# A planned attention and mixture-of-experts kernel: more buffers for the first loads, a shared port that the planner always knows, pooling sums moved from GpSimd to VectorE, and a new table of priorities

## The chip, the core and the metric

The kernel runs on one core of a Trainium2 chip. Five engines work side by side and wait for one another through semaphores: TensorE (PE in the rows, with PEld for its weight loads), VectorE (DVE), ScalarE (ACT), GpSimd (POOL) and SyncE (SP), which here only issues transfers. The metric is the device time of one execution in microseconds (us), lower is better. Of several runs the median is taken.

## The reference

Two stages follow each other. The first is an attention whose keys and values are one and the same: a map of 384 x 32 positions with 128 channels is averaged over 4 x 4 windows to 768 keys and multiplied by a 128 x 128 matrix. The second sends each of the 49,152 output rows to one of 8 experts.

```python
B, N, C = 4, 384 * 32, 128
kv_pool = kv.reshape(B, H // 4, 4, W // 4, 4, C).mean(axis=(2, 4))
k = v = kv_pool.reshape(B, -1, C) @ w_sr                  # 768 keys for each batch
a = softmax(q @ k.transpose(0, 2, 1) / sqrt(C))
x = (a @ v).reshape(B * N, C)                             # 49152 rows
logits = normalized(x) @ normalized(expert_emb).T / tau   # 8 experts
e = argmax(logits); gate = softmax(logits)[e]
out[row] = gate * (relu(x[row] @ w1[e]) @ w2[e])          # inner width 1024
```

## The kernel before

**Tiles and steps.** Attention runs in 96 steps `k` of 512 query rows, 24 steps to a batch. A step has four blocks `j` of 128 rows. For each block TensorE makes the 128 x 768 scores `s` (`s_mm`, L717, six matmuls: the operands are held as a high and a low float16 part, and three of the four products are taken), VectorE takes the row maximum (`s_max`, L722), one of two engines turns it into a bias (`s_bias`, L732 on ScalarE or L734 on VectorE), and ScalarE writes the exponentials `p` (`s_exp`, L740). Then `p` is split into a high part (`p_hi`, L758 on ScalarE or L760 on VectorE) and a low part (`p_lo`, L768 on VectorE or GpSimd), both are transposed by transfers, and TensorE multiplies them with the values (`av`, L813). For some blocks of the first steps `p` is transposed by TensorE instead (L403) and copied back (L784, L786), a choice of the strings in a table. A step ends with a division (`x_norm`, `x_mul`, L832 on ScalarE or L834 on VectorE) and rows for the experts.

**Experts.** Every four steps a chain of small VectorE operations picks experts and places, and GpSimd scatters the rows to DRAM, 128 rows in each indirect transfer. An expert tile `t` of 512 rows of one expert reads them back transposed, and goes through eight units `u`: `l1` (L1430, three matmuls of 512 columns into `ph`), `h_hi` on ScalarE (L1437, writes `hh`), `h_lo` on VectorE (L1442, writes `hl`), then `l2` (L1466 with `hh`, eight matmuls) and `l2_lo` (L1466 with `hl`, four). All eight units add up in one bank `po`, which VectorE empties in `o_out` (L1476). Its rows go out by scatters on GpSimd.

**Keys.** For batch 0 the map comes in 16 loads of 96 x 1024 numbers (`kv_load_0`, L455): four groups `h`, each of four rows `i` that VectorE adds up (`kv_sum_0`, L460; then `kv_cols_0`, L466 and L467). Seven buffers named `kvt0` hold them. For the other batches the map comes in eight loads of four rows each, added on GpSimd for batch 1 (`kv_adds`, L428) and by two VectorE reductions for batches 2 and 3 (`kv_window`, L446). From the pooled map TensorE makes the keys; a largest absolute value then gives their scale (for batch 0 in `kv_max_0`, L487).

**What sets the order.** Nothing is written in the order in which it runs. Every operation is handed to a planner with an engine, a duration, a priority (`key`) and what it depends on. `Plan.run` then plays the kernel through while it is built: the engine that is free first takes, of its ready operations, the one of lowest priority number, and the operation is put out then. So the durations and priorities in the code decide the fixed order of each engine's queue, and nothing else. The table `X` holds the offsets of the priorities and the strings that choose engines. Some operations carry `port=True`: GpSimd and VectorE are taken to hold one port in turn, but before the change only after 350 us of planned time (`X["pt"]`).

Of the kernel before, what the change touches and what calls it, by code (L numbers as in the profile page):

```python
# [33 lines left out]
P_LO = {"D": 0.96, "P": 1.65}  # L34
# [6 lines left out]
    ka=23, da=5.5, di=12.584, db=9.582, dma=1.426, ahead=2.462, av=10.242, av0=-0.17054466704045357, lb=0.8,  # L41
    l2=1.712, qt=5.48, lead=15.491, x=2.408, r=3.279, s=-1.285, p=9.158, x0=5.936, r0=8.101, s0=1.53, p0=5.53,
    qt0=0.531, pm="cabcbcacccbccbcacadcdad", pl="aaaaaaaa", nm="DDAAA", xn="ADAA", nm0="DDA", xn0="DA",
    we="dcdadcddaddcddcd", h=4.264, kv=6.773, kvs=0.752, w0=-14.986, start=22.623, early=22.314,
    wd=13.772691170763045, xw=1.904, qd=29, qs=7.744, ql=5.509,
    em="---------M-M-M-M-M-M-M-M-M-M-M-M-M-M-M-M-M", et=0.715, ec=0.5, v0=82.796, sd=0, qu=1.602, q0=-38.113,
    avd=0.262, m=1.928, end=-1.35, ne=-6.946, ge=-32, pt=350.0, kd=(2, 3), gap=1.8,
# [4 lines left out]
def attention_moe(  # L52
# [162 lines left out]
    LAT["~", "ACT"] = X["xw"]  # L215

# [15 lines left out]
    class Plan:  # L232
# [13 lines left out]
        def chain(self, key, step, fns, *deps, dur=0.17, eng="DVE", port=False):  # L246

            ops = []
            for i, fn in enumerate(fns):
                ops.append(self.add(eng, dur, key + i * step, fn, *(deps if not ops else ops[-1:]), port=port))  # L250
            return ops
# [14 lines left out]
        def run(self, begin):  # L266

            soon, now, free = {}, {}, {}
            held = dict(DVE=0.0, POOL=0.0)
# [20 lines left out]
            while any(count):  # L290
# [28 lines left out]
                if op.port and t > X["pt"]:  # L319
                    other = held["POOL" if eng == "DVE" else "DVE"]  # L320
                    if other > t + 0.1:
                        rest = [x for x in now[eng] if not x[2].port and self.can_go(x[2])]
                        rest = [x for x in rest if not (scatters(x[2]) and t < paced + X["gap"])]
                        if rest:
                            x = min(rest)
                            now[eng].remove(x)
                            now[eng].append((op.key, i, op))
                            heapq.heapify(now[eng])
                            op = x[2]
                        else:  # L330
                            t = other
# [110 lines left out]
    def kv_window(b, h, i):  # L442
        if i == 0:
            kv_pooled(b, h)
# [1511 lines left out]
```

## Time and profile before

| | us |
|---|---|
| median of 3 runs | 2136.58 |
| lowest and highest run | 2129.0, 2136.97 |
| the profiled execution, its own time | 2133.14 |
| span in its trace, first to last instruction | 2131.4 |
| TensorE busy | 1961.6 (92%) |
| VectorE busy | 1738.8 (82%) |
| ScalarE busy | 1551.0 (73%) |
| GpSimd busy | 1263.2 (59%) |
| mean granted clock of TensorE, as a share of full speed | 0.984 |

A share of the whole span is a mean over unlike stretches, so the rows below cut it: up to the first scores at 46 us, attention alone up to some 380 us, attention and expert tiles together up to some 1800 us, and experts alone at the end. Busy time of an engine includes time in which an instruction has begun and is held up.

### The profile page before, as it was taken

Reading aid. Unit: us, or ns where it says so; the run is one execution under the profiler, and the core shown is the slowest. Engines: PE = TensorE matmul, PEld = TensorE weight load, DVE = VectorE, ACT = ScalarE, POOL = GpSimd, SP = SyncE. Lnnn points to the kernel's source line nnn. Section 1 sums busy time; section 2 is a strip of 40 time slices with the busy share of each in tenths; the row PEclk is TensorE's granted clock in tenths of the full one; section 3 lists DMA queues with packets and bytes.
Section 4 is the critical chain, followed back from the end, with each engine's and each line's share of the span. In section 5 each row is a group of like instructions: output and inputs, shape, how many; then the busy total and the mean of one; then the engine's idle time right before and its main releaser. Section 6 shows DMA issues by size and latency. Waiting matters only on the chain. (4 is left out here: it accounts for less than half of the span.)

```text
span 2131.4 us, 57911 instructions
## 1 busy us (share of the span) xinstructions
PE 1961.6 (92%) x21396; PEld 1500.0 (70%) x21396; DVE 1738.8 (82%) x3711; ACT 1551.0 (73%) x3256; POOL 1263.2 (59%) x1744
## 2 busy tenths in 40 slices
PE   3777888899999999999999999999999999999997
PEld 1556676676776777677777777677777776776687
DVE  7989788789998888999988888788888887565554
ACT  3977788787877778688888887787888886543333
POOL 1558654566666667656557667656666656656333
PEclk9989899999999999999999999999999999999999
DMA  8987554999999999899888799797879777432242
GB/s 236 193 214 195 137 106 95 205 183 181 169 179 177 168 172 181 178 184 186 151 157 158 143 161 185 147 161 147 156 145 164 145 133 133 83 80 61 47 106 53
DMA packets 844545, 322.66 MB, mean 151 GB/s; under 512 B 792659, under 2 KB 804060, under 8 KB 842465
## 3 DMA queue, kind: packets, MB, share of 16 engines
q1 hardware_dynamic: 817184, 264.13, 67.1%
q0 software_dynamic: 24704, 53.53, 9.5%
q8 instruction: 170, 2.79, 0.5%
q10 hardware_dynamic: 2368, 1.25, 0.2%
q14 instruction: 119, 0.97, 0.2%
HBM read 170.55 MB, written 64.50 MB: 110 GB/s over the span
## 5 line engine op out<-in xcount | busy, mean ns | idle before, releaser
L1442 DVE SCALAR_TENSOR_TENSOR hl<-ph,hh 128x512 f16<-128x512 f32 x740 | 506.4, 686 | 176.4 <-ACT hh L1437 131.6
L190 POOL DMA_INDIRECT out_dram<-o,m x388 | 411.5, 1061 | 400.0 <-DVE o L1476 109.8
L1430 PE MATMUL ph<-x,wbuf 128*128 128x512 f16 (+1 forms) x2328 | 601.4, 370 | 21.4 <-DVE hl L1442 12.5
L1437 ACT ACTIVATE hh<-ph 128x512 f16<-128x512 f32 x740 | 439.3, 595 | 241.7 <-PE ph L1430 161.2
L190 POOL DMA_INDIRECT xs_rows<-rows,pi x384 | 429.0, 1117 | 214.8 <-issue 31.8
L1466 PE MATMUL po<-wbuf,hh 128*128 128x128 f16 x5920 | 452.5, 219 | 34.4 <-DVE o L1476 16.7
L717 PE MATMUL s<-k,qT 128*128 128x512 f16 (+1 forms) x2304 | 442.1, 331 | 32.1 <-ACT p L740 22.0
L740 ACT ACTIVATE p<-s,nm,qa 128x768 f32<-128x768 f32 x384 | 380.0, 991 | 98.5 <-DVE nm L734 71.8
L1466 PEld LDWEIGHTS <-hh 128*128 128x128 f16 x6208 | 381.3, 98 | 65.4 <-issue 30.1
L722 DVE TENSOR_REDUCE nm<-s 128x1 f32<-128x768 f32 x384 | 363.7, 948 | 28.2 <-PE s L717 17.7
L768 DVE TENSOR_TENSOR plo<-p,phi 128x768 f16<-128x768 f32 x339 | 339.5, 1002 | 25.0 <-ACT phi L758 16.0
L717 PEld LDWEIGHTS <-qT 128*128 128x128 f16 x2304 | 218.2, 99 | 166.5 <-issue 45.8
L1430 PEld LDWEIGHTS <-wbuf 128*128 128x128 f16 x2544 | 227.1, 98 | 144.3 <-issue 29.6
L813 PE MATMUL xp<-v,pthi 128*128 128x137 f16 x4200 | 313.0, 224 | 4.5 <-DVE w L600 1.3
L1466 PEld LDWEIGHTS <-hl 128*128 128x128 f16 x3104 | 228.7, 98 | 109.7 <-issue 3.3
L813 PEld LDWEIGHTS <-pthi 128*128 128x128 f16 x4200 | 274.8, 98 | 40.1 <-issue 6.1
L758 ACT CAST phi<-p 128x768 f16<-128x768 f32 x345 | 286.8, 832 | 6.9 <-issue 2.4
L1466 PE MATMUL po<-wbuf,hl 128*128 128x128 f16 x2960 | 286.4, 219 | 0.3 <-issue 0.2
L813 PE MATMUL xp<-v,ptlo 128*128 128x137 f16 x2100 | 187.2, 224 | 2.2 <-DMA ptlo<-plo 2.0
L813 PEld LDWEIGHTS <-ptlo 128*128 128x128 f16 x2100 | 142.0, 98 | 3.1 <-DMA ptlo<-plo 2.4
L846 POOL TENSOR_TENSOR rows<-x,rows 128x512 f16<-128x512 f32 x96 | 113.3, 1180 | 41.2 <-ACT rows L841 40.5
L861 ACT ACTIVATE junk<-x 128x128 f32<-128x128 f32 x384 | 116.3, 311 | 6.1 <-DVE x L834 5.1
(358 smaller groups left out, 1958.4 us busy)
## 6 DMA issues: line engine op xcount, KB each, us to landing
wbuf<-w_prep SPq DMA_DIRECT2D x106, 1026.0 KB
q<-in_q_dram SPq DMA_DIRECT2D x96, 256.0 KB
kvt<-in_kv_dram SPq DMA_DIRECT2D x24, 768.0 KB
wf<-in_moe_w_dram SPq DMA_DIRECT2D x16, 512.0 KB
out_dram<-o,m POOLq DMA_INDIRECT x388
kvt<-in_kv_dram SPq DMA_DIRECT2D x16, 384.0 KB
xs_rows<-rows,pi POOLq DMA_INDIRECT x384
w_prep<-wo SPq DMA_DIRECT2D x8, 514.0 KB
```

The costliest lines, as they stand in the source:

```text
L190: ins = nc.gpsimd.indirect_dma_start(out=dst[:, :], out_offset=bass.IndirectOffsetOnAxis(ap=idx, axis=0), in_=src, in_offset=None, bounds_ ...
L717: nc.tensor.matmul(t[:, lo:hi], qs[:, l, :], r[:, lo:hi], start=i == 0, stop=i == 2)
L722: V.tensor_reduce(out=nm, in_=ks[k]["s", j], axis=AX.X, op=ALU.max, negate=True)
L740: nc.scalar.activation(out=p, in_=ks[k].pop(("s", j)), func=AF.Exp, bias=ks[k].pop(("nm", j)), scale=ks[k]["fac"],)
L758: nc.scalar.copy(out=hi, in_=p)
L768: eng.tensor_tensor(out=lo, in0=ks[k].pop(("p", j)), in1=hi, op=ALU.subtract)
L813: nc.tensor.matmul(ks[k]["xp", h][:, i, :w], l[:, c, :], r[:, c, :w], start=n == 0, stop=n == len(terms) - 1)
L861: nc.scalar.activation(out=junk, in_=ks[k]["x"][:, j, 0:C], func=AF.Square, accum_out=groups[g]["ss"][:, i * NQ + j : i * NQ + j + 1],)
L1430: nc.tensor.matmul(ph[:, kk * n : (kk + 1) * n], wt[:, o + f : o + f + P], r, start=i == 0, stop=i == 2)
L1437: nc.scalar.activation(out=hh, in_=ts[t]["ph", u], func=AF.Relu)
L1442: V.scalar_tensor_tensor(out=hl, in0=ts[t].pop(("ph", u)), scalar=0.0, in1=ts[t]["hh", u], op0=ALU.max, op1=ALU.subtract)
L1466: nc.tensor.matmul(ts[t]["po"][:, j * C : (j + 1) * C], h[:, kk * n + j * P : kk * n + (j + 1) * P], wt[:, f : f + P], start=u == 0 and i ...
```

## The change

Six things change.

1. Of batch 0's 16 loads, the four of group `h = 1` use the four buffers `wf` of the experts' weights, and the last of group 3 uses `wo0`; the other eleven share the seven `kvt0`.
2. The planner applies the shared port from the start, on more operations (a list of names, `SHARED`, and more `port=True`), with a small gap after the other engine's hold, and a TensorE operation that begins after more than 2.05 us of idle time is planned as slower for a while.
3. The sums of the map for batches 1 to 3 are four additions on VectorE; GpSimd's five and VectorE's reductions are gone.
4. Durations: `p_lo`, the scatters, the copies, transposes and others are given other numbers.
5. New offsets and engine strings in `X`. Over the whole kernel, 89 of the bias operations move from VectorE to ScalarE, 36 of the divisions `x_mul` move there too (two instructions each on ScalarE, one on VectorE), and 45 of `p_hi` move from ScalarE to VectorE. Five steps (24 to 28) turn their queries by transfer and not by TensorE, which is 20 transposes of 128 x 128 fewer.
6. The chain that picks experts for the first three groups has an earlier priority, and the first selection of tiles runs on VectorE.

```diff
-P_LO = {"D": 0.96, "P": 1.65}
+P_LO = {"D": 0.9, "P": 1.62}
+SHARED = (
+    "halve", "guess", "square", "times", "update", "norm", "guard", "logits", "shift", "hits", "onehot", "pick", "cast",
+    "gate", "same", "take", "power", "floor", "after", "until", "divide",
+)
+KV_ADD = {"D": (1.13, 0.6, 0.33, 0.2), "P": (2.4, 1.25, 0.7, 0.45)}
...
-    l2=1.712, qt=5.48, lead=15.491, x=2.408, r=3.279, s=-1.285, p=9.158, x0=5.936, r0=8.101, s0=1.53, p0=5.53,
+    ka=23, da=6.087, di=12.327, db=9.098, dma=1.67, ahead=2.284, av=9.354, av0=0.067, lb=-0.963, l2=2.044, qt=8.333,
...
-                if op.port and t > X["pt"]:
-                    other = held["POOL" if eng == "DVE" else "DVE"]
-                    if other > t + 0.1:
...
                 if op.port:
-                    held[eng] = t + op.dur
-                op.end = t + op.dur
+                    mate = "POOL" if eng == "DVE" else "DVE"
+                    if held[mate] > t + 0.02:
+                        op.ready = asked[eng] = held[mate] + PORT[eng]
+                        put(op)
+                        continue
...
+                took = op.dur
+                if eng == "PE":
+                    if t - free.get(eng, 0.0) > 2.05:
+                        cold = t + 3.4
+                    took += max(min(op.dur, (cold - t) / 2), 0.0)
+                op.end = t + took
...
         return [
-            lambda: add(row(0), row(0), row(1)), lambda: add(row(2), row(2), row(3)),
-            lambda: add(row(0), row(0), row(2)), lambda: add(cols(0, 2), cols(0, 2), cols(2, 4)),
-            lambda: add(lambda: kv_pooled(b, h), cols(0, 1), cols(1, 2)),
+            add(rows(0, 2), rows(0, 2), rows(2, 4)), add(rows(0, 1), rows(0, 1), rows(1, 2)),
+            add(cols(0, 2), cols(0, 2), cols(2, 4)), add(lambda: kv_pooled(b, h), cols(0, 1), cols(1, 2)),
         ]
...
+    KV_BUFS = dict(kvt0=7, wf=4, wo0=1)
+
+    def kv_tag(h, i):
+        return "wf" if h == 1 else "wo0" if h == i == R - 1 else "kvt0"
...
-            if b in X["kd"]:
-                for i in range(2):
-                    r = add("DVE", 1.2, t0 + 8.0 + 0.2 * i, lambda h=h, i=i: kv_window(b, h, i), o, r, *deps)
-                    reads("kvt", r)
...
+            on = X["kd"][b - 1]
+            for i, fn in enumerate(kv_adds(b, h, V if on == "D" else nc.gpsimd)):
+                r = add(ENG[on], KV_ADD[on][i], t0 + 8.0 + 0.1 * i, fn, o, r, *deps, port=True)
+                reads("kvt", r)
```

How the change moves instructions is seen at three places.

**The start of SyncE's queue.** Here stand the loads of batch 0's map (`kvt_h_i`) and of the first queries (`q`), from the seventh row on. Before:

```order
L455 DMA kvt_1_2_193<-in_kv_dram 96x1024
L636 DMA q_197<-in_q_dram 128x512
L636 DMA q_199<-in_q_dram 128x512
L636 DMA q_206<-in_q_dram 128x512
L455 DMA kvt_1_3_213<-in_kv_dram 96x1024
L455 DMA kvt_2_0_217<-in_kv_dram 96x1024
L455 DMA kvt_2_1_224<-in_kv_dram 96x1024
L455 DMA kvt_2_2_238<-in_kv_dram 96x1024
L636 DMA q_244<-in_q_dram 128x512
```

And now, from the same place of the same queue:

```order
L468 DMA kvt_1_2_192<-in_kv_dram 96x1024
L468 DMA kvt_1_3_196<-in_kv_dram 96x1024
L468 DMA kvt_2_0_201<-in_kv_dram 96x1024
L468 DMA kvt_2_1_210<-in_kv_dram 96x1024
L468 DMA kvt_2_2_214<-in_kv_dram 96x1024
L468 DMA kvt_2_3_218<-in_kv_dram 96x1024
L468 DMA kvt_3_0_222<-in_kv_dram 96x1024
L468 DMA kvt_3_1_230<-in_kv_dram 96x1024
L649 DMA q_234<-in_q_dram 128x512
L468 DMA kvt_3_2_240<-in_kv_dram 96x1024
L468 DMA kvt_3_3_244<-in_kv_dram 96x1024
```

Before, six loads of queries stand ahead of the last load of the map, and now one does. The first two loads of expert weights follow the map's in both orders, now with one more load of queries between.

**One unit of an expert tile on TensorE.** In the long middle stretch, tile 11, from `l1` of unit 3 (`ph11_3`) to `l2` of the same unit (`hh11_3`); `hl11_1` is the low part of unit 1, and so on. One row stands for each run of matmuls. Before:

```order
L1430 MATMUL ph11_3_9497<-x_11_8486,wbuf2_4559 128x512
...
L1466 MATMUL po11_9469<-wbuf2_4559,hl11_1_9433 128x128
...
L1466 MATMUL po11_9469<-wbuf2_4559,hh11_2_9465 128x128
...
L1430 MATMUL ph11_4_9535<-x_11_8486,wbuf2_4559 128x512
...
L1466 MATMUL po11_9469<-wbuf2_4559,hl11_2_9478 128x128
...
L1466 MATMUL po11_9469<-wbuf2_4559,hh11_3_9525 128x128
```

And now (`s_0` are scores of attention):

```order
L1443 MATMUL ph11_3_9408<-x_11_8372,wbuf2_4404 128x512
...
L1479 MATMUL po11_9386<-wbuf2_4404,hh11_1_9289 128x128
...
L1479 MATMUL po11_9386<-wbuf2_4404,hl11_1_9317 128x128
...
L730 MATMUL s_0_159<-k0_1_4954,qT34_8903 128x512
...
L1443 MATMUL ph11_4_9447<-x_11_8372,wbuf2_4404 128x512
...
L1479 MATMUL po11_9386<-wbuf2_4404,hh11_2_9397 128x128
...
L1479 MATMUL po11_9386<-wbuf2_4404,hl11_2_9412 128x128
...
L1443 MATMUL ph11_5_9473<-x_11_8372,wbuf2_4404 128x512
...
L1479 MATMUL po11_9386<-wbuf2_4404,hh11_3_9426 128x128
```

Before, `l2` of unit 3 follows its `l1` after one other unit's `l1`, and between `hh` and `hl` of a unit lies an `l1`. Now `l2` follows after two other units' `l1` and a block of scores, and `hl` comes right behind `hh`. Of the 352 units of tiles 30 to 73 none stood nearer before than this one, and at least a tenth as near; now 95 in 100 stand at least as far apart as this one.

**The seam between two expert tiles on TensorE.** From the last matmuls of tile 10 (`hl10_7`) to the first `l2` of tile 11 (`hh11_0`), which needs the bank `po` that `o_out` of tile 10 has emptied. Before:

```order
L1466 MATMUL po10_9057<-wbuf1_4558,hl10_7_9341 128x128
...
L1430 MATMUL ph11_2_9441<-x_11_8486,wbuf2_4559 128x512
...
L717 MATMUL s_0_159<-k0_1_3981,qT34_8866 128x512
...
L1466 MATMUL po11_9469<-wbuf2_4559,hh11_0_9343 128x128
```

And now (`xp32_0` is a half step of `av`, 36 matmuls):

```order
L1479 MATMUL po10_8965<-wbuf1_4403,hl10_7_9245 128x128
...
L826 MATMUL xp32_0_9296<-v0_1_108,pthi32_0_8705 128x137
...
L826 MATMUL xp32_0_9296<-v0_1_108,ptlo32_0_8738 128x137
...
L730 MATMUL s_1_160<-k0_1_4954,qT34_8903 128x512
...
L1443 MATMUL ph11_2_9379<-x_11_8372,wbuf2_4404 128x512
...
L1479 MATMUL po11_9386<-wbuf2_4404,hh11_0_9267 128x128
```

Before, 9 matmuls lie in between, and now 45. Of the 44 seams of tiles 30 to 73 nearly all were like this one before; now three in four are, and the narrowest are as narrow as before.

## Rows read from the trace of the kernel before

**Rows 1.** Busy time by stretch: PE, PEld, DVE, ACT, POOL, granted clock, DMA share, GB/s.

```profile
0.00:30.00 30.00, 5.95 (x18) 3.51 (x18) 19.65 (x58) 11.35 (x24) 3.26 (x27) 1.00 0.95 246
...
46.00:380.00 334.00, 272.30 (x2269) 213.41 (x2268) 285.70 (x613) 260.64 (x539) 197.73 (x225) 0.92 0.69 160
...
400.00:1800.00 1400.00, 1356.70 (x15338) 1028.15 (x15338) 1221.44 (x2621) 1117.26 (x2386) 888.61 (x1264) 1.00 0.89 164
1800.00:2132.00 332.00, 303.87 (x3592) 239.69 (x3588) 186.78 (x368) 141.28 (x265) 158.84 (x206) 0.99 0.34 74
```

**Rows 2.** Timeline of the start: begin, duration (us), engine, line, what, idle before.

```profile
22.00 3.03 SPq L455 DMA_DIRECT2D kvt<-in_kv_dram  x5
...
34.39 1.22 DVE L460 TENSOR_TENSOR kvt<-kvt,kvt 96x1024 f32<-96x1024 f32 x1 [0.17 <-DMA kvt<-in_kv_dram]
...
39.98 0.55 DVE L487 TENSOR_REDUCE m<-s 128x1 f32<-128x384 f32 x1
...
45.89 0.80 PE L717 MATMUL s<-k,qT 128*128 128x512 f16 x2 [0.91 <-ACT k L523]
```

**Rows 3.** Who TensorE waited for, 46 to 380 us, then 400 to 2132.

```profile
PE s L717 <- ACT p L740: 20.6, 17, 2.6
...
PE po L1466 <- DVE o L1476: 16.7, 26, 2.0
PE po L1466 <- ACT hh L1437: 13.9, 20, 2.7
```

**Rows 4.** VectorE's groups, 46 to 380 us: busy us, mean ns, idle before.

```profile
L768 DVE TENSOR_TENSOR plo<-p,phi 128x768 f16<-128x768 f32 x46 | 49.9, 1085 | 4.9 <-ACT phi L758 4.1 <-issue 0.7
...
L665 DVE TENSOR_SCALAR qa<-qa,ksc 128x2 f32<-128x2 f32 x10 | 12.2, 1219 | 0.0
...
L1053 DVE TENSOR_TENSOR wo<-w 128x4 f32<-128x4 f32 x7 | 6.2, 889 | 0.0
```

**Rows 5.** Single lines, whole span: ns least/median/greatest, first and last start us.

```profile
L768 DVE TENSOR_TENSOR plo<-p,phi x339: 895/950/2717, 59.7 to 1828.7; 128x768 f16<-128x768 f32 x170
...
L665 DVE TENSOR_SCALAR qa<-qa,ksc x48: 207/221/4728, 44.6 to 1713.0; 128x2 f32<-128x2 f32 x48
...
L1053 DVE TENSOR_TENSOR wo<-w x8: 142/158/2097, 42.7 to 253.7; 128x4 f32<-128x4 f32 x8
...
L446 DVE TENSOR_REDUCE pooled<-kvt x32: 1867/1916/1952, 457.4 to 1041.1; 96x64 f32<-96x1024 f32 x32
...
L466 DVE TENSOR_TENSOR kvt<-kvt x4: 670/686/689, 12.3 to 35.6; 96x512 f32<-96x512 f32 x4
```

**Rows 6.** GpSimd's sums of the map for batch 1, 46 to 380 us.

```profile
L428 POOL TENSOR_TENSOR kvt<-kvt 96x512 f32<-96x512 f32 (+1 forms) x32 | 36.5, 1142 | 0.6
```

**Rows 7.** TensorE's timeline in the middle stretch; the spacing of starts is read.

```profile
801.15 0.81 PE L1430 MATMUL ph<-x,wbuf 128*128 128x512 f16 x3
801.80 0.39 PE L1466 MATMUL po<-wbuf,hl 128*128 128x128 f16 x4
802.03 0.61 PE L1466 MATMUL po<-wbuf,hh 128*128 128x128 f16 x8
802.47 1.14 PE L717 MATMUL s<-k,qT 128*128 128x512 f16 x6
803.45 0.89 PE L813 MATMUL xp<-v,pthi 128*128 128x137 f16 x12
...
804.54 0.81 PE L1430 MATMUL ph<-x,wbuf 128*128 128x512 f16 x3
```

**Rows 8.** Groups of the whole span that the table of engines moves or removes.

```profile
L403 PE MATMUL pq<-ident,q 128*128 128x128 f32 x116 | 18.6, 287 | 9.6 <-ACT q L671 5.4 <-DVE x L834 1.8 <-ACT x L832 1.4
...
L758 ACT CAST phi<-p 128x768 f16<-128x768 f32 x345 | 286.8, 832 | 6.9 <-issue 2.4
...
L732 ACT ACTIVATE nm<-nm,scales,qa 128x1 f32<-128x1 f32 x206 | 79.3, 385 | 51.1 <-DVE nm L722 42.7 <-issue 5.5 <-DVE qT L697 0.9
...
L832 ACT ACTIVATE x<-xp,rn 128x136 f32<-128x136 f32 x266 | 84.6, 371 | 48.8 <-DVE rn L824 30.3 <-DVE wo L1053 3.5 <-DVE rn L823 3.3
```

More of the change, by code (lines that the diff above doesn't have):

```diff
@@ L318, in run @@
                     continue
-                if op.port and t > X["pt"]:
-                    other = held["POOL" if eng == "DVE" else "DVE"]
-                    if other > t + 0.1:
[L322 to L331, printed above, removed]
-                if op.port:
-                    held[eng] = t + op.dur
-                op.end = t + op.dur
+                if op.port:
+                    mate = "POOL" if eng == "DVE" else "DVE"
[3 more added lines that the diff above has]
+                        continue
+                    rest = [x for x in now[eng] if not x[2].port] if eng == "POOL" and asked[mate] > t else []
+                    rest = [x for x in rest if self.can_go(x[2]) and not (scatters(x[2]) and t < paced + X["gap"])]
+                    if rest:
+                        x = min(rest)
+                        now[eng].remove(x)
+                        now[eng].append((op.key, i, op))
+                        heapq.heapify(now[eng])
+                        op = x[2]
+                    else:
+                        asked[eng] = 0.0
+                        held[eng] = t + op.dur
+                took = op.dur
[4 more added lines that the diff above has]
+                op.end = t + took
                 free[eng] = op.end
@@ L422, in kv_pooled, with kv_adds, rows @@
         return st[b]["pooled"][:, h, :]
-    def kv_adds(b, h):
+    def kv_adds(b, h, eng):
         def add(out, in0, in1):
-            nc.gpsimd.tensor_tensor(out=out(), in0=in0(), in1=in1(), op=ALU.add)
-        def row(i):
-            return lambda: st[b]["kvt", h][:, i, :]
+            return lambda: eng.tensor_tensor(out=out(), in0=in0(), in1=in1(), op=ALU.add)
+        def rows(lo, hi):
+            return lambda: st[b]["kvt", h][:, lo:hi, :]
         def cols(lo, hi):
@@ L1529, in kv_rows_0 @@
             for i in range(R):
-                o = took("kvt0", add("SP", 0.45, t0 + i, lambda h=h, i=i: kv_load_0(h, i), *turn("kvt0", 7), dma=1.3))
+                tag = kv_tag(h, i)
+                room = turn(tag, KV_BUFS[tag])
+                o = took(tag, add("SP", 0.45, t0 + i, lambda h=h, i=i: kv_load_0(h, i), *room, dma=1.3))
                 if i == 0:
-                    first, tile = o, len(uses["kvt0"]) - 1
+                    first, tile = o, uses[tag][-1]
                 else:
@@ L1809, in group_ops @@
             t -= X["ge"]
+        if g < 3:
+            t -= X["gk"]
         ops = g_logits(g)
-        lg = chain(
-            t, 0.3, ops, *counted[g], *placed.get(g - 1, ()), *placed.get(g - 2, ()), dur=0.22 if g > 3 else 0.17, port=True,
-        )
+        lg = chain(t, 0.3, ops, *counted[g], *placed.get(g - 1, ()), *placed.get(g - 2, ()))
         t += 0.3 * len(ops)
@@ L1828, in group_ops @@
         sc = [
-            add("POOL", 1.37, t + 1.37 * i, lambda i=i: g_scatter(g, i), pc[-1], gc[-1], dma=0.22) for i in range(GT)
+            add("POOL", 1.12, t + 1.37 * i, lambda i=i: g_scatter(g, i), pc[-1], gc[-1], dma=0.22) for i in range(GT)
         ]
```

88 lines of the change are left out of this document (45 added, 43 removed).

## The prediction

> **What bounds the kernel now.** I read the busy time by stretch first, then TensorE's waits, then VectorE's groups where TensorE is idle. The reader is to see three stretches with three different limits [rows 1]. From 400 to 1800 us TensorE is busy for 1356.7 of 1400 us: it is the bound, and only 43.3 us are idle there. At the end, 1800 to 2132, 28.1 us are idle. From 46 to 380, attention alone, it is busy for 272.3 of 334 us, so 61.7 us are idle, and its mean granted clock is 0.92, between its two levels of 1.2 and 2.4 GHz, after stretches in which it stood idle. At full clock those 272.3 us would be some 272.3 x 0.92 = 250.5, so the low level costs about 22 us more. No engine is full in that stretch: VectorE is at 285.7 of 334 (86%), ScalarE at 260.6 (78%). They wait for one another. Ahead of it the start costs 45.9 us until the first scores [rows 2].
>
> So the most that an order could give back is 61.7 + 22 in the first stretch, 43.3 + 28.1 behind it, and part of the start. The TensorE work itself hardly changes.
>
> **The start.** The first scores come at 45.89, 11.5 us after the last addition of batch 0's map begins at 34.39 [rows 2], and that addition waits for its transfer. The five last loads are issued only from 22.00 on. Ahead of the last load's landing the queue has 16 loads of 96 x 1024 x 4 bytes and six of queries of 128 x 512 x 4 bytes, 7.86 MB; at the 246 GB/s of the first 30 us [rows 1] this is 32.0 us, and the addition begins 2.4 us after that. Now one load of queries stands ahead: 6.55 MB, 26.6 us, and with the same 2.4 us the addition begins at 29.0, 5.4 us sooner. VectorE can follow: twelve additions of 1.22 us [rows 2] and four of 0.69 [rows 5] with smaller ones behind are under 20 us from the first landing on. But the largest of the keys (39.98 before) is queued on VectorE behind the two maxima of the first expert's weights, in both orders. Their loads land after 6.55 + 0.26 + 1.05 = 7.86 MB, which is one load of queries later than the map, and two query subtractions now stand there as well. The weights' loads now also wait until group 1 of the map has left their buffers; its additions end before the map's last load lands, so I count nothing. I take 4 of the 5.4 us. The bounds are 0, if the queries or VectorE's queue then come last, and 6.
>
> **The first stretch.** Here instructions of VectorE are held up. L665 works on two numbers per partition. Its median is 0.221 us and its longest 4.728 [rows 5], while its mean in this stretch is 1.219 [rows 4]. L665, L768 and L1053 together: 10 x (1.219 - 0.221) + 46 x (1.085 - 0.950) + 7 x (0.889 - 0.158) = 10.0 + 6.2 + 5.1 = 21.3 us of holding-up. These three alone are 6% of the stretch, and the plan for it counted none, since its port rule began at 350 us of planned time. GpSimd's additions, 36.5 us in 32 instructions of 1.14 us [rows 6], stand right there and are removed. VectorE gets in return eight times four additions: 1.22, 0.69, and two smaller ones that no row shows, bounded by 0 and 0.69 each. Going by halves (0.35, 0.20) a load costs 2.46 us and the batch 19.7. Up to the first expert unit VectorE's queue has 32 bias operations fewer (at 0.207, the least of L665, 6.6 us) and 8 high parts more (between 0 and 0.95, the median of L768; I take half, 4 us). So VectorE's own work grows by 19.7 - 6.6 + 4 = 17 us, and it has less to do only if more than 17 of the 21.3 us go. That would be worth little by itself.
>
> What I expect is less waiting by TensorE: its largest wait here is for the exponentials that free a score tile, 20.6 us in 17 waits [rows 3], and they come late when a VectorE instruction ahead of the maximum or the bias is held up. Shorter idle time also keeps the clock up. The price lies between a loss of the 17 us (over VectorE's 86% share, 20) and a gain of half of the 61.7 + 22. I take a gain of 10, an eighth of it, because VectorE's own work grows, and because the old plan already got 82% from a wrong rule.
>
> **Behind it.** Two of TensorE's waits go by the distances in its queue. The seam: `l2` waits for `o_out`, 16.7 us in 26 waits, the longest 2.0 [rows 3]. Nine matmuls fill it before, one block of `l1` and one of scores: 0.65 + 0.98 = 1.63 us by their spacing [rows 7]. Now two blocks of `av` stand there too, (804.54 - 803.45) = 1.09 each, so 3.81 us. That is 2.18 us more, above the longest wait. The unit: `l2` waits for `hh`, 13.9 us in 20 waits, the longest 2.7. Before, 0.23 + 0.44 + 0.65 + 0.23 = 1.55 us of matmuls lie between `l1` and `l2` of a unit; now 0.44 + 0.23 + 0.98 + 0.65 + 0.44 + 0.23 + 0.65 = 3.62, that is 2.07 more. So nearly all of the 30.6 us could go. `hl` now comes right behind `hh`, but with 3.62 + 0.44 = 4.06 us after its `l1`, where VectorE has its time. What is late next: a faster TensorE asks more of VectorE (1221 of 1400 us, 87%) and ScalarE (80%) [rows 1]. ScalarE gets some 60 bias operations at 0.385 and 72 division parts at 0.371, and loses some 35 high parts at 0.832 [rows 8]: 23.1 + 26.7 - 29.1 = 21 us more, 81% of the 1400. VectorE loses what these were there, and two reductions of 1.916 for each load of batches 2 and 3 [rows 5], 30.7 us a batch against 19.7. No engine becomes the bound, but their queues are full enough to be late elsewhere. I take half of the 30.6, 15; the bounds are 0 and 31.
>
> Twenty transposes of queries fewer on TensorE, at 18.6 / 116 = 0.16 us [rows 8]: 3 us. The transfers that take their place stand in SyncE's queue steps ahead. The earlier experts' chain and the first selection on VectorE cost nothing that I can find: TensorE's queue has the first expert unit behind the same attention work as before.
>
> **A rule weighed.** The reductions of batches 2 and 3 show no holding-up: 1867 to 1952 ns in 32 instructions. An operation with two inputs in SBUF, L768, shows it: 895 to 2717 [rows 5]. The Trainium skill (SBUF — State Buffer, Who interferes with whom) states that a reduction never contends with GpSimd, while an addition of two SBUF inputs is blocked by a GpSimd instruction that reads SBUF; the rows agree. By that rule alone, were each of the 64 additions of these batches to meet a whole GpSimd sum of 1.14 us, VectorE would stand 73 us longer in its 1400, at 91% in place of 86% (1221 - 22 + 73), and the waits of TensorE that I count as gone would come back: the forecast would be 15 us higher. By L768's own excess in the first stretch, 0.135 us, the 64 cost 9 us on an engine that isn't the bound, and the sum stays as it is. I follow the row.
>
> **Sum.** 4 + 10 + 15 + 3 = 32 us. The profiled execution took 2133.1, so 2101; that execution lies 3.4 us below the median of 2136.58 and inside the three runs, and I leave the forecast at 2101.
>
> **Rivals.**
> *VectorE bounds the first stretch, slower.* The additions bring 17 us of work, and the weights' low parts, rows and scatters of GpSimd keep holding the port, so the 21.3 us stay. At VectorE's 86% share the stretch grows by 17 / 0.86 = 20 us, and the waits behind it return nothing. 2133 + 20 - 4 - 3 = 2146. It decides when less than 17 of the 21.3 us go. For it: VectorE is the fullest engine there. Against: GpSimd's 32 sums, 36.5 us, are gone from that stretch [rows 6]. Chance 0.13. The Trainium skill's rule above, on additions of two inputs, is the mechanism.
> *Nothing but the transposes counts.* The start is given back, since the attention alone then waits for exponentials as before, and at the seam `hl` or the scores come late in place of `o_out` and `hh`. 2133 - 3 = 2130. For it: VectorE and ScalarE are at 80 to 87%, and an engine works its queue in order. Against: both distances grew by more than the mean of the waits (0.64 and 0.70 us). Chance 0.20.
> *The first stretch heals.* Idle time and low clock feed each other, and half of 61.7 + 22 goes, with all of 30.6: 2133 - 4 - 42 - 31 - 3 = 2053. For it: no engine is full there. Against: VectorE gets 17 us more of its own work. Chance 0.15.
>
> **How the numbers follow.** The forecast, 2101, has 0.52, with 2085 to 2117 as its own range. For 8 in 10 I go down to 2066, halfway to the healing case, and up to 2140, which takes in the case of no effect and leaves out half of the slower one. A change of 0.5% (11 us) is what a measurement of this kernel can tell from none: faster than 2126 or slower than 2147. Faster: 0.52 + 0.15 and a quarter of the 0.20, 0.72. Slower: half of the 0.13 and a little of the rest, 0.10. Same: 0.18.
>
> **What would show it.** First scores near 42 us. In the stretch after it, L665 near its median of 0.221 and TensorE's idle time under 55 us, with the granted clock above 0.92. Between 400 us and the end, waits for `o_out` and `hh` under 15 us together. I'd be wrong if VectorE's instructions are held up for as long as before, or if `hl` takes over the waits.

## The result and the profile after

| | before | after |
|---|---|---|
| median of 4 runs, us | 2136.77 | 2062.41 |
| lowest and highest run, us | 2129.0, 2142.09 | 2059.74, 2073.14 |
| span of the profiled execution, us | 2131.4 | 2058.8 |
| TensorE busy in it, us | 1961.6 (92%) | 1931.3 (94%) |

The changed kernel is faster: ratio 0.9664, 95% interval 0.9618 to 0.9710. The forecast was 2101 with a range of 2066 to 2140, so the direction was right and the time lies 3.6 us below the range.

Line numbers of the changed kernel are 4 higher near its top and 13 or 14 higher behind the sums of the map (L665 is now L678, L768 L781, L1053 L1066). I cut both traces at the same two events, the first scores and the first `l1` of an expert tile. Busy time by stretch, after (columns as in rows 1):

```profile
0.00:30.00 30.00, 4.04 (x10) 1.73 (x10) 18.44 (x46) 2.90 (x6) 3.25 (x27) 1.00 0.95 231
44.50:325.60 281.10, 247.72 (x2240) 196.02 (x2240) 259.57 (x621) 255.02 (x555) 137.52 (x141) 0.99 0.84 189
325.60:2058.80 1733.20, 1672.25 (x19101) 1277.29 (x19100) 1416.59 (x3012) 1276.17 (x2791) 1061.53 (x1512) 1.00 0.80 150
```

The same two stretches before:

```profile
45.90:378.90 333.00, 271.39 (x2265) 213.13 (x2265) 284.70 (x612) 259.87 (x537) 197.19 (x224) 0.92 0.69 159
378.90:2131.40 1752.50, 1677.88 (x19096) 1279.71 (x19096) 1423.07 (x3013) 1276.18 (x2692) 1061.91 (x1493) 1.00 0.79 147
```

Of the 72.6 us between the spans, the start gave 45.9 - 44.5 = 1.4, the first stretch 333.0 - 281.1 = 51.9 and the rest 19.3. In the first stretch TensorE's busy time fell by 23.7 us at nearly the same instructions, mostly because the granted clock is 0.99 and not 0.92, and its idle time fell from 61.6 to 33.4.

VectorE's groups in the first stretch, after (busy us, mean ns; compare rows 4):

```profile
L781 DVE TENSOR_TENSOR plo<-p,phi 128x768 f16<-128x768 f32 x44 | 44.2, 1004 | 0.2
L442 DVE TENSOR_TENSOR kvt<-kvt 96x1024 f32<-96x1024 f32 (+2 forms) x24 | 18.4, 766 | 0.0
...
L1066 DVE TENSOR_TENSOR wo<-w 128x4 f32<-128x4 f32 x7 | 2.5, 353 | 0.0
...
L678 DVE TENSOR_SCALAR qa<-qa,ksc 128x2 f32<-128x2 f32 x10 | 2.1, 210 | 0.0
```

The scale of the queries (L678) takes 0.210 us in place of 1.219. The holding-up that I counted as 21.3 us is, by the same medians, 44 x 0.054 + 7 x 0.195 = 3.7. VectorE is now at 92% of this stretch.

Who TensorE waited for, after, from 44.6 to 325.6 us, and then from 330 us on:

```profile
PE s L730 <- DVE pw L799: 7.3, 8, 3.0
PE s L417 <- ACT p L753: 6.9, 8, 2.3
PE s L730 <- ACT p L753: 6.7, 11, 1.2
...
PE ph L1443 <- DVE hl L1455: 23.2, 40, 1.4
...
PE po L1479 <- DVE o L1489: 1.3, 1, 1.3
...
PE po L1479 <- ACT hh L1450: 0.3, 1, 0.3
```

Before, beside rows 3, from 400 us on:

```profile
PE ph L1430 <- DVE hl L1442: 12.5, 13, 3.7
```

The wait for exponentials (20.6 us in rows 3) is 6.7. Behind, `o_out` went from 16.7 to 1.3 and `hh` from 13.9 to 0.3, while `hl` grew from 12.5 to 23.2.

### The profile page after: what moved, and what is told of

It reads as the page before. It is cut to its first block, busy times and chain, and to the rows that moved or that the text cites. A ratio compares the mean times of both kernels' runs of the same rounds, so it can differ in the third digit from the quotient of the medians.

```text
span 2058.8 us, 58042 instructions
## 1 busy us (share of the span) xinstructions
PE 1931.3 (94%) x21376; PEld 1479.9 (72%) x21376; DVE 1706.2 (83%) x3715; ACT 1543.2 (75%) x3367; POOL 1203.0 (58%) x1679
## 5 line engine op out<-in xcount | busy, mean ns | idle before, releaser
L1443 PE MATMUL ph<-x,wbuf 128*128 128x512 f16 (+1 forms) x2328 | 599.3, 369 | 30.6 <-DVE hl L1455 23.2
L194 POOL DMA_INDIRECT out_dram<-o,m x388 | 416.3, 1073 | 335.9 <-DVE o L1489 71.6
L194 POOL DMA_INDIRECT xs_rows<-rows,pi x384 | 437.3, 1139 | 229.1 <-issue 35.5
L1479 PEld LDWEIGHTS <-hh 128*128 128x128 f16 x6208 | 408.8, 98 | 161.7 <-issue 3.8
L735 DVE TENSOR_REDUCE nm<-s 128x1 f32<-128x768 f32 x384 | 363.5, 947 | 16.0 <-PE ph L1443 6.9
L1443 PEld LDWEIGHTS <-wbuf 128*128 128x128 f16 x2544 | 230.7, 98 | 169.8 <-issue 44.6
L781 DVE TENSOR_TENSOR plo<-p,phi 128x768 f16<-128x768 f32 x340 | 330.5, 972 | 11.0 <-ACT phi L771 7.7
L730 PEld LDWEIGHTS <-qT 128*128 128x128 f16 x2304 | 213.9, 98 | 135.1 <-issue 28.7
L826 PEld LDWEIGHTS <-pthi 128*128 128x128 f16 x4200 | 266.6, 97 | 16.5 <-issue 12.7
L771 ACT CAST phi<-p 128x768 f16<-128x768 f32 x300 | 249.8, 834 | 3.5 <-DMA pthi<-phi 0.7
L845 ACT ACTIVATE x<-xp,rn 128x136 f32<-128x136 f32 x338 | 108.0, 371 | 187.9 <-DVE rn L837 145.1
L1479 PEld LDWEIGHTS <-hl 128*128 128x128 f16 x3104 | 205.9, 98 | 2.6 <-issue 1.4
L745 ACT ACTIVATE nm<-nm,scales,qa 128x1 f32<-128x1 f32 x295 | 114.1, 388 | 43.0 <-DVE nm L735 30.1
```

Of the source, the lines that this page charges most:

```text
L194: ins = nc.gpsimd.indirect_dma_start(out=dst[:, :], out_offset=bass.IndirectOffsetOnAxis(ap=idx, axis=0), in_=src, in_offset=None, bounds_ ...
L730: nc.tensor.matmul(t[:, lo:hi], qs[:, l, :], r[:, lo:hi], start=i == 0, stop=i == 2)
L735: V.tensor_reduce(out=nm, in_=ks[k]["s", j], axis=AX.X, op=ALU.max, negate=True)
L745: nc.scalar.activation(out=nm, in_=nm, func=AF.Identity, scale=ks[k]["fac"], bias=scales[:, 3:4])
L771: nc.scalar.copy(out=hi, in_=p)
L781: eng.tensor_tensor(out=lo, in0=ks[k].pop(("p", j)), in1=hi, op=ALU.subtract)
```

## The experiments

The runs fell on several chips. The kernel before took 2137 to 2144 us beside some of them and 2090 to 2091 beside the last six, so ratios to the kernel before on the same chip are compared, not times. The expected times are for a kernel before at 2137 us. The length of the first stretch hardly depends on the chip: four kernels with the changed kernel's order up to there show 281.1, 280.0, 281.9 and 283.0 us (e17, v3 and e8), and two with the order of the kernel before 333.0 and 330.6 (e10). So differences of up to 3 us there mean nothing. The part behind does depend on it, so it is compared only where the kernel before took about the same.

| kernel | ratio (95%) | first scores | first `l1` | first stretch | behind |
|---|---|---|---|---|---|
| before | 1 | 45.9 | 378.9 | 333.0 | 1752.5 |
| changed | 0.9664 (0.9618 to 0.9710) | 44.5 | 325.6 | 281.1 | 1733.2 |
| e1_port_late | 0.9761 (0.9728 to 0.9794) | 44.1 | 350.7 | 306.6 | 1736.0 |
| e2_sums_pool | 0.9868 (0.9833 to 0.9904) | 43.8 | 378.1 | 334.3 | 1731.2 |
| e4_before_pt0 | 1.0109 (1.0072 to 1.0145) | 45.8 | 394.2 | 348.4 | 1772.9 |
| e6_new_table | 0.9855 (0.9820 to 0.9890) | 44.6 | 363.5 | 318.9 | 1727.1 |
| e5_before_kd1 | 1.0031 (1.0014 to 1.0048) | 45.7 | 376.5 | 330.8 | 1764.9 |
| e3_old_table | 1.0017 (1.0001 to 1.0033) | 47.0 | 374.7 | 327.7 | 1762.7 |
| e8_old_dist | 0.9687 (0.9665 to 0.9709) | 45.1 | 328.1 | 283.0 | 1755.3 |
| e10_before_dist | 0.9943 (0.9922 to 0.9963) | 46.0 | 376.6 | 330.6 | 1754.2 |
| e13_no_sums | 0.9727 (0.9702 to 0.9751) | 42.9 | 344.8 | 301.9 | 1727.5 |
| e11_old_strings | 0.9666 (0.9641 to 0.9692) | 43.6 | 345.6 | 302.0 | 1716.4 |
| e12_gk0 | 0.9763 (0.9738 to 0.9788) | 43.1 | 355.0 | 311.9 | 1731.4 |
| e7_nocold | 0.9763 (0.9738 to 0.9789) | 42.2 | 350.1 | 307.9 | 1748.4 |
| e17_small | 0.9698 (0.9680 to 0.9715) | 43.7 | 323.7 | 280.0 | 1697.5 |
| e18_before_small | 0.9920 (0.9897 to 0.9944) | 46.5 | 356.8 | 310.3 | 1711.2 |
| e14_measured | 0.9800 (0.9782 to 0.9818) | 45.1 | 350.6 | 305.5 | 1701.8 |
| e16_measured_before | 1.0041 (1.0022 to 1.0059) | 46.2 | 378.2 | 332.0 | 1710.9 |
| e15_nudge | 0.9741 (0.9722 to 0.9759) | 43.7 | 336.1 | 292.4 | 1699.6 |
| v3_mix | 0.9660 (0.9637 to 0.9683) | 42.6 | 324.5 | 281.9 | 1694.0 |

The last four columns are of one profiled execution each, in us. My theory was that GpSimd's sums of batch 1's map held the port and that moving them off freed the first stretch. The rivals were the rule that the planner applies from the start, and the new table.

**Rule, sums, table: one taken away, or one alone.**

Without the rule before 350 us:

```diff
-                if op.port:
+                if op.port and t > 350.0:
```

> The changed kernel, but the planner applies the shared port only after 350 us of planned time, as before; everything else (table, sums on VectorE, durations, buffers) stays. If the rule from the start is what emptied the first stretch of waits, the bias on VectorE there comes back toward a mean of 1.0 us (0.210 with the rule), TensorE's idle time in the first stretch rises from 33 toward 55 us, and the time is 2090 to 2115. If the sums that left GpSimd did it, VectorE's instructions stay short without the rule, and the time is 2060 to 2072. If the table did it, also 2060 to 2075, with some longer VectorE instructions that cost TensorE nothing.

Measured: 2084.9 us, first stretch 25.5 us longer. The scale of the queries (L678, which the expectation calls the bias) took 0.401 us on average, not near 1. The time lies between the cases, nearer to the rule's, and the sign that I named didn't come; what 25 us are worth is seen from e14 below.

Batch 1's sums on GpSimd again:

```diff
-kd="DDD"
+kd="PDD"
```

> The changed kernel, but batch 1's sums of the map (32 additions, about 4.8 us planned per load) stand on GpSimd again; batches 2 and 3 stay on VectorE. If the rule is the cause, the planner works round them: VectorE's bias stays under 0.4 us in the first stretch and the time is 2060 to 2078, perhaps even a little less since VectorE is rid of 20 us of work. If the sums' place is the cause, the stretch gets back most of its loss: 2095 to 2115, and the bias on VectorE near 1 us.

Measured: 2109.0 us, as the sums' place had it and not the rule: the whole first stretch is back at 334.3 us although the planner knows the port. The sign of the sums' place failed, though: the scale (L678) took 0.265 us on average, not near 1, and the order is another one here too. The rows of one place tell how the sums can cost time. Up to 146 us it keeps pace with the changed kernel (228 matmuls of scores begun, for 222). Then, in the timeline of VectorE, GpSimd, ScalarE and TensorE:

```profile
147.88 2.27 DVE L946 TENSOR_TENSOR d<-x,mx 128x128 f32<-128x128 f32 x1
150.08 1.28 DVE L602 TENSOR_SCALAR w_t<-ident,w_t 2x2 f32<-2x2 f32 x1
...
147.68 4.47 POOL L442 TENSOR_TENSOR kvt<-kvt 96x1024 f32<-96x1024 f32 x3 [1.21 <-DMA kvt<-in_kv_dram]
152.22 0.45 POOL L442 TENSOR_TENSOR pooled<-kvt 96x128 f32<-96x128 f32 x1
...
152.71 1.15 ACT L1083 ACTIVATE wo<-wf,w 128x1024 f16<-128x1024 f32 x1 [4.96 <-POOL pooled L442]
...
151.42 0.58 PE L607 MATMUL w_m<-w_t,ones 2*128 2x2 f32 x2 [5.15 <-DVE w_t L602]
152.48 5.85 PE L818 MATMUL xp<-v,pw 128*128 128x137 f32 x24 [0.48 <-DVE w L613]
```

While GpSimd adds from 147.7 to 152.2, an operation of VectorE whose median in this trace is 0.280 us takes 2.27, and the next, of 0.210, takes 1.28. TensorE waits 5.15 us for that small one, and the 24 matmuls behind it run at the low clock (granted 0.50 from 152.4 to 158.4 us, the level of 1.2 GHz). From 145 to 165 us, e2 and then the changed kernel:

```profile
145.00:165.00 20.00, 11.02 (x50) 9.30 (x50) 11.97 (x20) 7.47 (x17) 12.89 (x14) 0.67 0.45 113
```

```profile
145.00:165.00 20.00, 16.01 (x112) 11.31 (x111) 19.78 (x40) 18.16 (x34) 14.54 (x14) 1.00 0.83 208
```

TensorE does 50 matmuls in place of 112. GpSimd's queue also waits 1.21 us for a load of the map ahead of its sums, and ScalarE waits 4.96 us for a sum to end.

The old rule from 0 us, alone in the kernel before:

```diff
-pt=350.0
+pt=0.0
```

> The kernel before, with one number changed: the old port rule holds from 0 and not from 350 us of planned time. If knowing the port early is the cause, the first stretch shortens by 25 to 45 us and the time is 2092 to 2112. If the sums or the table are the cause, GpSimd's sums still hold the port and 2136 moves by less than 10 us either way.

Measured: 2159.3 us, 1.1% slower, against both cases. The first stretch is 348.4 us. With the old table and GpSimd's sums, a planner that knows the port from the start made a worse order.

The new table alone in the kernel before:

```diff
 X = dict(
-    ka=23, da=5.5, di=12.584, ... kd=(2, 3), gap=1.8,
+    ka=23, da=6.087, di=12.327, ... kd=(1, 2, 3), pt=350.0, gap=1.8,
```

> The kernel before with the new table of offsets and engine strings alone (batch 1's sums as VectorE reductions, port rule from 350 us, old durations, old buffers, old chain of experts). If the table carries the gain, the time is 2075 to 2100. If the rule carries it, the first stretch keeps 50 us or more of idle time of TensorE, and only what the distances behind gave comes: 2110 to 2140. A table made for one planner can also fit another badly: over 2140 would say that table and rules only work together.

Measured: 2102.7 us, between the first two cases. It gives 14.1 of the 51.9 us in the first stretch (with batch 1's sums as reductions of VectorE). Behind, the profiled execution shows all of what the change gave, but it lies 10 us below the median; by the ratio, 31 us in all, some 16 us are left for the part behind.

Batch 1's sums as reductions, alone in the kernel before:

```diff
-kd=(2, 3)
+kd=(1, 2, 3)
```

> The kernel before with one change: batch 1's sums are made by VectorE's reductions, as those of batches 2 and 3 already are (16 of 1.9 us, 30 us of VectorE's time), and GpSimd has none. If GpSimd's sums are what held VectorE and, through it, TensorE, the first stretch shortens by 20 to 40 us from 333 although VectorE gets 30 us more, and the time is 2098 to 2118. If they only hurt together with the new table, 2130 to 2145. If VectorE is the bound of the first stretch, it grows by 30 us: 2160.

Measured: 0.3% slower than before, the second case: no gain from the place of the sums with the old table, and none of the 30 us of VectorE's work lost either, since the first stretch is 330.8.

The old table in the changed code:

```diff
 X = dict(
-    ka=23, da=6.087, ... kd="DDD", gk=66.84, tg=0.0, tl=9.893, gap=1.8,
+    ka=23, da=5.5, ... kd="DDD", gk=0.0, tg=0.0, tl=0.0, gap=1.8,
```

> The changed kernel with the old table of offsets and strings; sums on VectorE, the port rule from the start, the new durations and buffers stay, and the first experts' chain has no earlier priority. If sums and rule carry the first stretch, it stays near 290 us and only the distances behind are lost: 2080 to 2095. If the table has to fit the rule, 2110 to 2145.

Measured: 0.2% slower than before, the second case. Sums and rule without the new table give nothing: 327.7 us in the first stretch, and behind it the waits for `o_out` and `hh` are back.

**The distances of the expert unit.**

```diff
-lb=-0.963, l2=2.044, ... h=9.732
+lb=0.8, l2=1.712, ... h=4.264
```

> The changed kernel with three of the old offsets, those that set the distances between the parts of an expert unit: the high part's, and the two that set when l2 and its low part stand (4.264, 1.712 and 0.8 in place of 9.732, 2.044 and -0.963). By the prediction's step the waits for hh and o_out come back, half of 30.6 us or all of it: TensorE's idle time behind the first expert unit rises by 15 to 30 us, and the time is 2075 to 2092. If the rest of the table gave the 19 us behind, 2060 to 2070.

```diff
-lb=0.8, l2=1.712, ... h=4.264
+lb=-0.963, l2=2.044, ... h=9.732
```

> The kernel before with the three new offsets of the expert unit alone. By the prediction's step the waits for hh and o_out fall from 30.6 us to a few, and the part behind the first expert unit shortens from 1752.5 by 10 to 25 us: 2112 to 2127. If the offsets only work with the other priorities, hl or scores are late in their place: 2130 to 2150.

TensorE's longest waits in e8, whole run, and under it in e10:

```profile
PE po L1479 <- ACT hh L1450: 18.6, 33, 2.2
...
PE po L1479 <- DVE o L1489: 11.0, 22, 1.7
PE ph L1443 <- DVE hl L1455: 9.1, 10, 3.0
```

```profile
PE ph L1430 <- DVE hl L1442: 34.6, 40, 3.8
...
PE po L1466 <- DVE o L1476: 7.4, 16, 2.0
```

The offsets do what the prediction said: with the old ones the waits for `hh` and `o_out` come back (29.6 us), with the new ones alone in the kernel before they fall from 30.6 to 7.4. But `hl` moves the other way, 23.2 to 9.1 in e8 and 12.5 to 34.6 in e10. Net, these three waits are worth 18.6 + 11.0 + 9.1 - 23.2 - 1.3 - 0.3 = 13.9 us in the changed kernel, and 12.5 + 30.6 - 34.6 - 7.4 = 1.1 in the kernel before. The times agree in direction, not in size. Up to the first `l1` each has the order of the kernel that it was made from, so the ratios price the distances alone: 0.9687 for 0.9664 in e8 is some 5 us, with intervals that overlap, at the upper edge of the case in which the rest of the table gave the gain, and 0.9943 for 1 in e10 is some 12 us, the first case. TensorE's idle time behind the first `l1` rose by 13.7 us in e8, under the 15 that I named, and didn't fall in e10 (76.8 for 74.6); both ran beside a kernel before of 2144 us.

**Work left out, and other parts of the change.**

```diff
             for i, fn in enumerate(kv_adds(b, h, V if on == "D" else nc.gpsimd)):
+                if b == 1 and i < 3:
+                    continue
```

> The changed kernel with three of the four additions of each of batch 1's eight loads left out (so its keys are not the reference's); 18.4 us of VectorE's time in the first stretch go, nothing moves to GpSimd. If VectorE, at 92% there, is now the bound, the first stretch shortens by 12 to 20 us and the time is 2040 to 2052. If TensorE's own waits and the order decide, it moves by less than 8 us: 2054 to 2070. In the prediction's terms this prices the 17 us of VectorE's work by itself.

Measured: 2078.1 us, worse than both cases. The planner, with less to place, chose another order, and the first stretch is 20.8 us longer with 13.0 us less of VectorE's work.

```diff
-pm="cabcbcccccbacbcaaccbbab", pl="abaaaaaa", nm="ADAAA", xn="AAAA", nm0="DAA", ...
+pm="cabcbcacccbccbcacadcdad", pl="aaaaaaaa", nm="DDAAA", xn="ADAA", nm0="DDA", ...
```

> The changed kernel with the old engine strings (which engine makes each bias, division, high part, copy and weight product) and the new offsets. If the move of 89 biases and 36 divisions to ScalarE is what let VectorE take the sums, the first stretch grows by 10 to 30 us: 2080 to 2105. If the offsets are what matters in the table, 2062 to 2075.

Measured: 2064.5 us. The first stretch is 20.9 us longer, the part behind 16.8 us shorter than in the changed kernel's trace. The stretch is as long as the first case had it, the time is the second's: in time, the strings aren't needed for the gain.

```diff
-sd=1, ... gk=66.84
+sd=0, ... gk=0.0
```

> The changed kernel without the earlier priority of the first three groups' expert chains, and with the first selection of tiles on GpSimd again. The prediction gave this item nothing: 2058 to 2068. If the first expert unit waits for the chain, it comes later than 325.6 us by 5 to 20 and the time is 2068 to 2085.

```diff
-                    if t - free.get(eng, 0.0) > 2.05:
+                    if t - free.get(eng, 0.0) > 1e9:
```

> The changed kernel, whose planner no longer counts a TensorE operation as slower after idle time. If the clock in the first stretch heals because idle time is short, the clock stays at 0.97 or more and the time is 2060 to 2075. If the plan needs this rule to stay in step with the chip, the first stretch gets 10 to 30 us longer, with a clock under 0.97: 2072 to 2095.

Measured: 2086.9 and 2088.4 us, first stretches of 311.9 and 307.9, the clock in the second at 0.95. Both come out as, or 2 us above, the case in which the part matters; the prediction had the first of the two at nothing. Five different edits (e1, e7, e11, e12, e13) now gave 302 to 312 us. So I doubted that each of them showed its own part, and asked what any other order costs.

**The same order, and an order that is another for no reason.**

Changed kernel, every queue in the same order, batch 1's sums shrunk (e18 does the same to GpSimd's sums of the kernel before, with 16 columns):

```diff
-            return lambda: st[b]["kvt", h][:, lo:hi, :]
+            return lambda: st[b]["kvt", h][:, lo:hi, : 8 if b == 1 else None]
...
```

> The changed kernel with every queue in the same order; the first three additions of each of batch 1's loads work on 8 or 16 columns per row (its keys are not the reference's), so that some 14 to 16 us of VectorE's time go from the first stretch and nothing moves. If VectorE's work in this stretch is on the path, the stretch shortens by 8 to 16 us: 2045 to 2055. If its queue has slack at these places, 2056 to 2063.

> The kernel before with every queue in the same order; the first four additions of each of batch 1's loads on GpSimd work on 16 columns (its keys are not the reference's), so GpSimd no longer holds the port there. If the holding of the port by these sums is what made TensorE wait, the first stretch shortens by 15 to 35 us at the same order: 2100 to 2120. If other instructions of GpSimd hold VectorE up as much, or the order itself made TensorE wait, under 8 us: 2128 to 2137.

The first stretch of e17, then of e18, and two of e18's groups there:

```profile
43.70:323.70 280.00, 248.48 (x2239) 196.47 (x2239) 244.83 (x621) 255.16 (x554) 133.58 (x141) 0.99 0.84 190
```

```profile
46.50:356.80 310.30, 263.25 (x2264) 208.06 (x2264) 264.44 (x610) 258.45 (x536) 168.75 (x222) 0.95 0.76 171
```

```profile
L665 DVE TENSOR_SCALAR qa<-qa,ksc 128x2 f32<-128x2 f32 x10 | 4.0, 398 | 0.0
...
L428 POOL TENSOR_TENSOR kvt<-kvt 96x16 f32<-96x16 f32 x32 | 8.6, 270 | 2.3 <-DMA kvt<-in_kv_dram 1.7
```

In e17 VectorE has 14.7 us less to do, and the stretch is 1.1 us shorter, less than runs of this order differ by. So the sums' own work on VectorE costs next to nothing, at 92% busy. In e18 nothing but GpSimd's additions got short, 36.5 to 8.6 us, and the stretch is 22.7 us shorter, the scale (L665) at 0.398 us in place of 1.219. VectorE's busy time fell by 284.7 - 264.4 = 20.3 us, about as much as the stretch, with all its work still there. So GpSimd's sums cost the kernel before some 20 to 23 us of this stretch by what they held up. The times: 0.9920 for e18, 2090 x 0.008 = 17 us (12 to 22 by its interval), and 0.9698 for e17, which can't be told from the changed kernel's ratio. Both ran on the chip where the part behind is shorter for all. GpSimd's own queue is also 27.9 us shorter in e18; in the kernel before only one wait for these sums stands in this stretch, 3.5 us of ScalarE, so this matters little beside the port.

Which of TensorE's waits went in e18? Before and then e18, in this stretch:

```profile
PE s L717 <- ACT p L740: 20.6, 17, 2.6
PE w_m L594 <- DVE w_t L589: 7.7, 3, 5.3
```

```profile
PE s L717 <- ACT p L740: 18.7, 18, 2.6
...
PE w_m L594 <- DVE w_t L589: 2.8, 3, 1.9
```

The wait for exponentials hardly fell. What fell is the wait for a scale of the expert weights (`w_t`) and many smaller ones, and with the clock the busy time, by 8.1 us. The wait for exponentials follows the table: 15.9 to 20.6 us in all seven kernels with the old offsets, 11.3 or less in every one with the new, wherever the sums stand (10.0 in e2).

Planned durations set to what the traces show, changed kernel and kernel before, and one offset moved:

```diff
-KV_ADD = {"D": (1.13, 0.6, 0.33, 0.2), ...
+KV_ADD = {"D": (1.21, 0.68, 0.41, 0.28), ...
```

> The changed kernel, with the planned durations of batch 1's to 3's additions set to what the trace measured (1.21, 0.68, 0.41, 0.28 for 1.13, 0.60, 0.33, 0.20). If a truer plan makes a better order, 2050 to 2062. If any other order costs 20 to 30 us in the first stretch, as the runs so far suggest, 2075 to 2095 with a first stretch of 300 to 312 us.

```diff
-zip(kv_adds(b, h), (1.25, 1.25, 1.25, 0.7, 0.45))
+zip(kv_adds(b, h), (1.27, 1.27, 1.27, 0.72, 0.47))
```

> The kernel before, with the planned durations of GpSimd's additions set to their medians in the trace (1.27 three times, 0.72 and 0.47 for 1.25, 0.7 and 0.45). If the kernel before also stands at an order that its table was made for, any other one costs it 10 to 30 us: 2145 to 2165. If its first stretch is no better than other orders of the same rules, 2130 to 2143.

```diff
-x0=4.37
+x0=4.6
```

> The changed kernel with one offset of the first steps moved by 0.23 us (x0, the priority of the rows for the experts, 4.37 to 4.60). The queues are the same up to step 10 and others behind. If any other order costs 20 to 30 us, the first stretch is 300 to 312 us and the time 2075 to 2095. If only real parts of the change matter, 2058 to 2066.

The first stretches of e14 and e15:

```profile
45.10:350.60 305.50, 257.12 (x2204) 200.83 (x2204) 269.40 (x628) 257.42 (x557) 141.09 (x148) 0.95 0.75 173
```

```profile
43.70:336.10 292.40, 252.88 (x2205) 199.90 (x2205) 265.35 (x628) 257.44 (x557) 142.11 (x146) 0.97 0.78 180
```

Truer durations cost the changed kernel 24.4 us in the first stretch, and an offset moved by 0.23 us costs 11.3, less than the 20 to 30 that I had named for any other order. The kernel before loses nothing there by the same kind of edit (332.0 for 333.0 in its shortest execution; its ratio is 0.4% up, some 9 us, at the lower edge of the case in which it loses). As far as these few runs show, its order was an ordinary one of its kind, and the changed kernel's is an uncommonly good one.

Old strings from step 23 on:

```diff
-nm="ADAAA", xn="AAAA"
+nm="DDAAA", xn="ADAA"
...
-        return P_MODES[pm[i] if i < len(pm) else rest[i % len(rest)]]
+        return P_MODES[pm[i] if i < len(pm) else "a" if k >= KA else rest[i % len(rest)]]
```

> The changed kernel, with the old engine strings for bias, division and high parts only from step 23 on, where the expert units begin; up to there every queue has the same order. With the old strings throughout, the part behind the first expert unit was 16.8 us shorter (1716.4 for 1733.2) and the first stretch 20.9 longer. If the two can be had together, 2040 to 2052. If the part behind depends on its order like the first stretch does, anything from 2052 to 2075.

Measured: 0.9660, which can't be told from the changed kernel's 0.9664. The first stretch stayed, as expected (281.9). Behind it is 1694.0 us, 3.5 less than in e17, which has the changed kernel's order and ran beside the same 2090 us; so e11's 16.8 us were not those of these three strings. No run beats the changed kernel beyond doubt.

## Why the prediction was off

**The start, 4 predicted, 1.4 measured.** The transfers did most of what was said. The last addition of batch 0's map begins at 31.17, 3.2 us sooner than in rows 2 (I said 5.4): the first 30 us moved 231 GB/s and not 246, and at that rate 6.55 MB take 28.4 us, which with the 2.4 behind them gives 30.8. Timeline of VectorE, after:

```profile
31.17 1.21 DVE L473 TENSOR_TENSOR kvt<-kvt,kvt 96x1024 f32<-96x1024 f32 x1
...
33.98 2.33 DVE L1053 TENSOR_REDUCE wm<-wf 128x1 f32<-128x1024 f32 x2
...
37.55 0.56 DVE L500 TENSOR_REDUCE m<-s 128x1 f32<-128x384 f32 x1 [0.21 <-PE s L492]
```

The largest of the keys still stands behind the two maxima of the first expert's weights, and then came 2.4 us sooner (39.98 before), of which 1.4 reached the first scores. No run took the new buffers away alone. The old buffers go with first scores at 44.6 to 46.5 us, the new ones with 42.2 to 47.0.

**The first stretch, 10 predicted, 51.9 measured: this step failed.** VectorE's short operations were held up, and TensorE's clock fell, as said. Three judgments were wrong. The first was the price of VectorE's own work, 17 us against the gain; e17 puts the sums' 14.7 us at 1.1. I read it so, without a run of its own: the sums have a low priority and stand where VectorE has time, while a held-up operation stands wherever GpSimd happens to add, as the 5.15 us of TensorE in e2 show. The second was the eighth of 61.7 + 22. Removing the holding by GpSimd's sums alone gives 22.7 (e18; 17 by the times), about twice the forecast for this stretch, where VectorE's busy time fell by about the same amount: what holds VectorE up went into the stretch nearly one for one. The clock rose with it, from 0.92 to 0.95. The third was the path: I had the held-up operations reach TensorE by late exponentials, but without GpSimd's holding 18.7 of those 20.6 us stay (e18), and only the kernels with the new offsets are rid of about half of them or more. The remaining 29 are a difference, not a run. I put them down to the order: with the old table they are not had (e3, 327.7), and two changes of no meaning lose 11 and 24 of them (e14, e15). How much of the 29 is in the table's values and how much in their fit to this one plan stays open, and so does the worth of the rule by itself: taking it out costs 25.5 (e1), hardly more than e14.

**Behind, 15 + 3 = 18 predicted, 19.3 measured.** The exchange was the one named: the distances removed 16.7 + 13.9 - 1.3 - 0.3 = 29.0 us of waits, `hl` took back 23.2 - 12.5 = 10.7, and 18.3 stay. e8 and e10 show it in both directions. But that the size came out is in part luck. TensorE's idle time behind the first `l1` fell by 74.6 - 60.9 = 13.7 us only and its busy time by 5.6, and by their ratios the distances alone are worth some 5 us in the changed kernel (e8, not clear of nothing) and 12 in the kernel before (e10). What gave the rest of the 19.3 isn't shown; the three us for the transposes can't be separated from it.

**The rule weighed.** The Trainium skill (SBUF — State Buffer, Who interferes with whom) says that a VectorE instruction with two SBUF inputs contends with a GpSimd one that reads SBUF, for shared ports that it calls an exclusive lock. e2's 2.27 us for such an operation of 0.280 agrees. The prediction weighed the rule against VectorE's new additions; in the changed kernel's trace their means are 1.21, 0.68, 0.41 and 0.28 us in the first stretch and 1.21, 0.68, 0.42 and 0.29 behind it, so none was held up for long, and the sums that left GpSimd were the ones that did the blocking.

**The rivals.** "The first stretch heals" (2053, chance 0.15) was the nearest, 9 us low: it took 42 for the first stretch and 31 behind. "VectorE bounds the first stretch" and "Nothing but the transposes counts" fell with the result, the first also with e17.

## What to carry to other kernels

Price an operation that holds a shared port by what it holds up on the critical chain, not by the busy share of the engine that is held: taking away 27.9 of the 36.5 us of GpSimd's sums gave 22.7 us in the stretch and 17 in the time, and 14.7 of the 18.4 us of the same sums on a VectorE at 92% gave about 1. Where a planner fixes the order, take parts out with the order kept (shrink the operands) and beside that change the order for no reason; otherwise a loss of 20 us from re-planning reads like the worth of the part. A wait removed by distance in one queue is paid in part by the next operand that is late there, so count what comes back, and check it by the time: here the waits and the ratios didn't agree in size.

## What was not expected of the hardware

The same program differs by chip: the kernel before took 2137 to 2144 us on some and 2090 on another. A nearly equal one (e16) shows there 332.0 us in the first stretch, for 333.0, but 1710.9 behind it, for 1752.5. The changed kernel's order (e17) shows 1697.5 behind it, for 1733.2. TensorE's weight loads waited there less for what the profile doesn't show, before and then e16, from 380 us on:

```profile
PEld L1466 <- issue: 33.5, 60, 2.2
PEld L1430 <- issue: 27.5, 52, 3.8
```

```profile
PEld L1466 <- issue: 21.8, 37, 2.0
PEld L1430 <- issue: 11.8, 20, 1.7
```

What it is stays open; an effect of 2% between kernels on different chips says nothing.
